# Attention and a gated feed-forward block on one core: an early dummy exponential and a new order table

## The chip, the cores and the metric

The kernel runs on one core of a Trainium2 chip. The metric is the device time of one execution in microseconds; the number compared is the median of several runs.

## What is computed

There are 4 batches of 12 heads; a sequence has 448 positions, a head 64 channels. Causal attention gives X (448 x 768 per batch), and X goes through a feed-forward block whose hidden values (1024) are gated by a convolution of three taps along the sequence. All in float32.

```python
scores = scale * np.matmul(q, k.transpose(0, 1, 3, 2))
scores = np.where(mask, -1000000000.0, scores)
attn = np.exp(scores - np.max(scores, axis=-1, keepdims=True))
attn = attn / (np.sum(attn, axis=-1, keepdims=True) + 1e-09)
out = np.matmul(attn, v)                      # 12 heads side by side are x
...
h = np.maximum(x @ w_in, 0.0)                 # 768 -> 1024
conv_out = sum over k of conv_w[k] * h shifted by k - 1 along the sequence
gate = 1.0 / (1.0 + np.exp(-conv_out))
return (h * gate @ w_out)                     # 1024 -> 768
```

## The kernel before

**Pairs of heads.** Work goes by pairs of heads, 24 of them, six to a batch, numbered from 0. A pair is five kinds of steps. TensorE makes transposed scores in blocks of 64 queries (`scores`, line 457) into four PSUM banks, as a whole or in two halves. VectorE adds the mask and takes the row minimum of the negated scores (`least`, line 492; in the trace a custom instruction and a read of its accumulator). ScalarE takes the exponential and the row sums (`expo`, line 498). TensorE transposes the probabilities (line 557) into the two banks of the ring `PT`, and ScalarE or VectorE copies them out (line 566). TensorE then multiplies with V (`times_v`, line 587). In the first batch the division by the row sums is applied to the product, by way of small matmuls that spread the reciprocals (line 603); in the others to the probabilities (line 529, "normalisation" below), after a sum (line 514) and a reciprocal (line 517). Two halves of the product are copied out and added (lines 646 and 650). From batch 1 on the product takes the two `PT` banks, so that the next transposes wait until both are copied out.

**Float32 at the speed of a rounded format.** Each operand of the feed-forward block is split into a rounded first part (lines 329, 330 and 333 for ScalarE, VectorE and POOL) and a second part, the rest (line 344, VectorE or POOL); a product is three matmuls of 448 columns, high by high, high by low, low by high. The weights come in 16 chunks each of W_in and W_out through three or more buffers, are scaled (line 369) and put together (line 372) before they are split.

**Feed-forward.** A first product (`ffn1`, line 903) sums nine matmuls of a kind over six pairs of X, then come relu, three taps, tanh and the gate (`activate`, lines 919 to 939). A second product (`ffn2`, line 961) is 24 matmuls to an output tile; ScalarE copies it out (line 972) and SyncE stores it. Batch 0 and 1 run beside the attention of the next batches: 144 first and 144 second matmuls for each, called "products" below. Batches 2 and 3 share the first half in `joint` (line 783), which uses seven instead of eight block products: it needs sums of weights and sums of X blocks (line 680) and adds results from PSUM (line 820). The 288 second products of both come last.

**What sets the order.** All steps are given to `Plan`, which writes the program: `run` goes through the steps that can be issued, estimates for each when it could start on each engine that may do it (`LAG`, `OWN`, `EXTRA` and a cost in ns per step; steps marked `port` take turns at a modelled port that VectorE and POOL share), and issues the one with the lowest rank. A rank is the start plus a lateness that the step was given, plus an entry of the table `OFFSET`, by kind and number of the step. `FROM` holds the time from which an engine counts as free. `PACE` gives for each pair of the last two batches how many products must have been issued before its scores and its product with V may be (through `progress`). The program has no scheduler at run time: each engine runs its list in order and waits on semaphores. `setup` (line 308) fills the mask, the identity and zeros; eight matmuls on zeros keep TensorE at work meanwhile.

Of the kernel before, what the change touches and what calls it, by code (L numbers as in the profile page):

```python
# [14 lines left out]
AF = mybir.ActivationFunctionType  # L15
# [8 lines left out]
class Plan:  # L24
# [8 lines left out]
    OWN = {"PE": 0, "DVE": 115, "ACT": 145, "POOL": 40, "SP": 0}  # L33
    EXTRA = {"PE": 100, "POOL": 42}
    WEIGHT = {"DVE": 1.15, "ACT": 1.0, "POOL": 0.5}
    FROM = {"PE": 3800.0, "SP": 500.0}
    ISSUE = {}
    OFFSET = {
        "PT": {11: -250, 12: -19050, 14: 100, 16: -50, 18: -19350, 19: -350, 20: -100, 21: -19500, 22: -200, 23: 100, 5: -100,
            9: -2750},  # L40
        "after": {5: 12750},
        "c12": {1: 4050},
        "c21": {3: 1550},
        "c22": {0: 100, 2: 18700},
        "chain": {140: 20000, 159: 7950, 189: 18150, 19: 850, 191: 3250, 206: 5600, 21: 600, 218: 5750, 236: 14150, 25: 650,
            34: 2050, 51: 1550, 57: 4850, 8: 1600, 96: 12050},
        "cw": {0: 350},
        "exp": {0: -100, 10: -9650, 14: 150, 16: -11250, 19: -400, 20: 1100, 4: -50, 5: -12250, 7: 50, 9: -100},
        "g": {(1, 0): -50, (1, 1): 100, (1, 2): -100, (1, 5): -250, (1, 6): -950, (1, 7): -250, (2, 1): 50, (2, 5): -50, (2,
            7): 50, (3, 0): 2050, (3, 4): 5550, (3, 5): 4450, (3, 7): 20000},  # L50
        "least": {0: -8300, 10: 1050, 13: 250, 14: 1400, 18: 500, 21: -1000, 22: -10850, 23: -450, 6: -500, 8: 400, 9: 100},
# [11 lines left out]
        "raw": {14: 1200, 16: 4150, 18: 3500, 19: 4500, 2: 3500, 23: 3600, 4: 450, 6: 1250, 8: 1000, 9: 5450},  # L63
        "rb": {5: 150},
        "s1": {1: 1100, 2: -14050},
        "s3": {0: -13750, 1: 1350, 2: 1100},
        "s4": {0: 100, 1: -250, 2: -100, 3: 9550},
        "scores": {10: 100, 13: -350, 22: 1950, 4: -10400, 9: 100},
        "sum": {(3, 0): -100},
        "t1": {0: 400, 1: 250, 2: -13650},  # L70
        "t1f": {1: 550, 2: -500},
        "t2": {1: -150, 2: 200},
        "t2f": {1: -1950},
        "t3f": {1: -4000},
        "t4": {0: -7800, 1: -19500, 2: -2250},
        "t4f": {1: -6350},
        "u2": {2: 1250},
        "vraw": {19: -3300, 2: -6400, 22: 1550, 3: 700, 4: 800, 5: 5200, 6: -11550, 9: -700},
# [4 lines left out]
    }  # L83
    SWITCH = {(0, 1): 90, (0, 2): 90, (3, 1): 90, (3, 2): 90, (1, 2): 95, (2, 1): 95, (1, 0): 200, (2, 0): 200, (1, 3): 100, (2, 3): 100, (0, 3): 20}

# [131 lines left out]
def attn_ffn_kernel(ctx: ExitStack, tc: tile.TileContext, qk, v, w_in, conv_w, w_out, out):  # L217
# [8 lines left out]
    nc = tc.nc  # L226
    P = 128
    B, NPAIR, _, _, S = qk.shape
# [40 lines left out]
    negm = many(2, [P, 8], F32, "negm")  # L269
    ssum = many(2, [P, 8], F32, "ssum")  # L270
# [38 lines left out]
    def setup():  # L309
        nc.gpsimd.memset(bank_zeros, 0.0)  # L310
        idle(bank[7], 8)
        nc.gpsimd.memset(mask, 0.0)
        for j in range(2):
            last = mask[64 * j : 64 * j + 64, S - 64 : S]
            nc.gpsimd.affine_select(
                out=last, in_=last, compare_op=ALU.is_ge, fill=-1.0e30,
                base=0, pattern=[[-1, 64]], channel_multiplier=1,
            )
        make_identity(nc, ident)
        for t in tops:  # L320
            nc.vector.memset(t, 0)
        for t in plan.rings["hr"]:
            nc.vector.memset(t[0][:, 0:1], 0.0)
            nc.vector.memset(t[0][:, S + 1 : S + 2], 0.0)
# [660 lines left out]
    LATE = 100  # L985
    SUM_LATE = 300
    PACED1 = False
    PACE = [-90 + 24 * i for i in range(2 * NPAIR + 1)]
    IN_AT = [(2, 3, 4, 4, 5)[i * 5 // NW] for i in range(NW)]
    OUT_AT = [i * NPAIR // NW for i in range(NW)]  # L990
    with tc.manual_schedule():
# [66 lines left out]
```

## Time and profile before

| what | value |
|---|---|
| median of 3 runs | 380.22 us (380.15 to 380.59) |
| the profiled execution | 381.26 us, of which 379.5 us are the span of the trace |
| mean granted TensorE clock | 0.998 of full speed |
| TensorE busy | 365.5 us, 96% of the span |
| VectorE, ScalarE, POOL busy | 279.3, 253.1, 158.2 us |
| DMA | 37.55 MB, 99 GB/s on the mean |

A share of busy time is an average over stages with different limits; which wait counts is read from the stage in which it stands. A wait is put down to the event that came last by the profile. In the rows L498 is line 498 of the kernel before; the kernel with the change has the same code four lines higher behind the setup (L494).

### The profile page before, as it was taken

How to read it: one execution, taken by the hardware profiler on the slowest of the kernel's cores; microseconds unless marked ns; L12 is line 12 of the kernel's file. 1: busy time of each engine (PE TensorE's matmuls, PEld its weight loads, DVE VectorE, ACT ScalarE, POOL GpSimd, SP SyncE). 2: the span in 40 equal slices, each digit the busy share in tenths (PEclk: the TensorE clock that was granted, in tenths of full speed). 3: DMA queues.
4: the chain of work that ended last, by engine and by line, in shares of the span. 5: the costliest groups of instructions: out<-in, count | busy, mean ns of one | idle time of the engine just before them, and what ended most of it. 6: DMA issues, size and time to landing. Idle time of an engine off the chain costs nothing.

```text
span 379.5 us, 8931 instructions
## 1 busy us (share of the span) xinstructions
PE 365.5 (96%) x3367; PEld 305.9 (81%) x3367; DVE 279.3 (74%) x762; ACT 253.1 (67%) x697; POOL 158.2 (42%) x187
## 2 busy tenths in 40 slices
PE   7999998999999999999999999899899899999996
PEld 3767766798898887888887888778699799999995
DVE  4788868878888767787968677769989898645500
ACT  2899898999871578978889988479544246434121
POOL 2257676545530042334247895841113902314600
PEclk9999999999999999999999999999999999999999
DMA  8997114342565252231204331310000000111021
GB/s 275 406 355 247 57 44 139 113 140 83 156 208 188 74 162 66 84 134 36 80 4 146 104 122 42 107 61 26 3 0 0 2 0 0 50 48 50 2 97 48
DMA packets 15163, 37.55 MB, mean 99 GB/s; under 512 B 1808, under 2 KB 4880, under 8 KB 15120
## 3 DMA queue, kind: packets, MB, share of 16 engines
q1 hardware_dynamic: 15120, 36.99, 28.8%
q8 instruction: 26, 0.43, 0.5%
q14 instruction: 17, 0.14, 0.1%
HBM read 31.47 MB, written 5.51 MB: 97 GB/s over the span
## 4 chain that ended last, share of the span: by engine, by line
PE 60%; DVE 14%; ACT 11%; issue 6%; POOL 5%; DMA 3%; POOLq 0%; ACTq 0%; DVEq 0%; SPq 0%
PE bank L961 23%; PE bank L903 9%; PE bank L557 7%; PE bank L587 7%; PE bank L457 7%; PE bank L783 6%; ACT p L498 4%; DMA wraw<-in_w_out_dram 3%; ACT parts L329 2%; DVE u L926 2%; DVE bank L492 2%; POOL wol L344 2%; DVE top L680 1%; POOL parts L344 1%; DVE parts L344 1%
## 5 line engine op out<-in xcount | busy, mean ns | idle before, releaser
L961 PE MATMUL bank<-parts,woh 128*128 128x448 f32 x384 | 112.7, 371 | 0.5 <-DVE woh L330 0.5
L498 ACT ACTIVATE p<-bank,negm 128x192 f32<-128x192 f32 (+6 forms) x168 | 78.9, 490 | 9.1 <-DVE negm L492 7.8
L961 PEld LDWEIGHTS bank<-parts,woh 128*128 128x128 f32 x384 | 71.0, 188 | 6.3 <-DVE woh L330 0.8
L492 DVE CUSTOM_DVE_ANT_0 bank<-bank,mask 128x384 f32<-128x384 f32 (+6 forms) x168 | 66.2, 452 | 7.5 <-PE bank L457 7.0
L961 PE MATMUL bank<-parts,wol 128*128 128x448 f32 x192 | 70.9, 369 | 0.0
L903 PE MATMUL bank<-parts,wih 128*128 128x448 f32 x192 | 58.4, 377 | 0.1
L557 PE MATMUL bank<-ident,p 128*128 128x128 f32 x336 | 51.0, 279 | 5.2 <-ACT p L498 1.9
L344 POOL TENSOR_TENSOR parts<-u,parts 128x448 fp32r<-128x448 f32 x37 | 43.8, 1188 | 19.9 <-ACT parts L329 17.8
L926 DVE SCALAR_TENSOR_TENSOR u<-hr,cw,u 128x448 f32<-128x448 f32 x64 | 45.8, 731 | 6.2 <-ACT u L939 5.3
L557 PEld LDWEIGHTS bank<-ident,p 128*128 128x128 f32 x336 | 38.3, 140 | 14.7 <-issue 3.3
L566 ACT COPY pt<-bank 128x512 f32<-128x512 f32 (+1 forms) x74 | 38.5, 541 | 14.8 <-PE bank L557 13.4
L457 PE MATMUL bank<-raw 64*64 64x128 f32 (+5 forms) x768 | 46.9, 362 | 0.6 <-DVE u L623 0.6
L333 POOL TENSOR_SCALAR parts<-u 128x448 fp32r<-128x448 f32 x21 | 12.9, 614 | 81.2 <-DVE u L932 45.1
L783 PE MATMUL bank<-parts,wih 128*128 128x448 f32 x150 | 42.9, 367 | 1.4 <-DVE hr L814 1.4
L587 PE MATMUL bank<-pt,vraw 64*64 64x64 f32 (+3 forms) x960 | 43.1, 317 | 0.0
L587 PEld LDWEIGHTS bank<-pt,vraw 64*64 64x64 f32 x960 | 31.0, 133 | 15.0 <-issue 8.2
L457 PEld LDWEIGHTS bank<-raw 64*64 64x64 f32 x768 | 30.2, 135 | 14.5 <-issue 7.2
L961 PEld LDWEIGHTS bank<-parts,wol 128*128 128x128 f32 x192 | 36.1, 188 | 3.2 <-DVE wol L344 0.5
L903 PEld LDWEIGHTS bank<-parts,wih 128*128 128x128 f32 x192 | 35.0, 188 | 3.0 <-DVE parts L344 0.3
L529 ACT ACTIVATE p<-p,rcp 128x256 f32<-128x256 f32 (+6 forms) x75 | 34.8, 514 | 3.7 <-DVE rcp L517 3.6
L498 ACT ACTIVATION_READ_ACCUMULATOR p<-bank,negm 128x1 f32 x168 | 36.9, 219 | 0.0
L903 PE MATMUL bank<-parts,wil 128*128 128x448 f32 x96 | 36.1, 376 | 0.0
(90 smaller groups left out, 549.5 us busy)
## 6 DMA issues: line engine op xcount, KB each, us to landing
raw<-in_qk_dram SPq DMA_DIRECT2D x24, 448.0 KB, 4.7
vraw<-in_v_dram SPq DMA_DIRECT2D x24, 320.0 KB, 3.0
wraw<-in_w_in_dram SPq DMA_DIRECT2D x16, 383.8 KB, 7.3
wraw<-in_w_out_dram SPq DMA_DIRECT2D x16, 383.8 KB, 3.5
out_dram<-u SPq DMA_DIRECT2D x24, 224.0 KB, 1.9
wraw<-in_conv_w_dram SPq DMA_DIRECT2D x1, 23.8 KB, 4.9
```

What stands on the lines that cost most here:

```text
L344: engine.tensor_tensor(out=out(), in0=src(), in1=f32(hi()), op=ALU.subtract)
L457: nc.tensor.matmul(at(s)[half(j ^ (k in SWAPPED)), to : to + k1 - k0], lhsT=t[:, 1, 64 * k : 64 * k + 64], rhs=t[:, 0, k0:k1], start=True, ...
L492: nc.vector.tensor_tensor_reduce(out=t, in0=t, in1=mask[:, S - 64 : S - 64 + n] if k == 2 else mask[:, S - n : S], scale=-0.125, scalar=3. ...
L498: nc.scalar.activation(at(t)[:, h : h + n], at(s)[:, o : o + n], AF.Exp, bias=negm[g % 2][:, c : c + 1], scale=-1.0, accum_out=ssum[g % 2] ...
L529: mul(t, t, rcp[g % 2][:, c : c + 1])
L557: nc.tensor.matmul(to, lhsT=p, rhs=ident, is_transpose=True)
L566: copy(at(part)[:, o : o + n], at(pt)[:, :n])
L587: nc.tensor.matmul(at((pv, r))[half(j), q0:q1], lhsT=at(vraw)[half(r), c if c < 3 else 3 + (c - 3) // 2, j], rhs=t[half(r), :, j], start=c ...
L783: nc.tensor.matmul(at(bank)[:, :S], lhsT=weights(w)[:, c], rhs=at(operands[c])[:, part], start=q == 0, stop=q == len(prods) - 1,)
L903: nc.tensor.matmul(at(ph)[:, :S], lhsT=block(w, NCC * f + cc), rhs=at(x)[:, part], start=q == 0, stop=q == len(prods) - 1)
L926: nc.vector.scalar_tensor_tensor(out=t, in0=src, scalar=w, in1=t, op0=ALU.mult, op1=ALU.add)
L961: nc.tensor.matmul(at(po)[:, :S], lhsT=block(w, NF * m + f), rhs=at(g)[:, part], start=q == 0, stop=q == len(prods) - 1)
```

## The change

Three things change. In `setup` VectorE sets the 8 columns of `negm[0]` to zero and ScalarE takes their exponential into `ssum[0]`, which later instructions overwrite. `PACE` starts 30 later and rises by 22 instead of 24 for each pair. The table `OFFSET` is another one throughout, and `FROM` lets the plan count ScalarE as free from 3500 ns on. Costs, lags and rules of the plan are the same.

```diff
-    FROM = {"PE": 3800.0, "SP": 500.0}
+    FROM = {"PE": 3800.0, "SP": 500.0, "ACT": 3500.0}
     ISSUE = {}
     OFFSET = {
-        "PT": {11: -250, 12: -19050, 14: 100, 16: -50, 18: -19350, 19: -350, 20: -100, 21: -19500, 22: -200, 23: 100, 5: -100,
-            9: -2750},
...
+        "PT": {10: -100, 11: 250, 14: -500, 15: -11650, 18: -11650, 19: 200, 20: -150, 21: -100, 6: -7550},
...
         make_identity(nc, ident)
+        nc.vector.memset(negm[0], 0.0)
+        nc.scalar.activation(ssum[0], negm[0], AF.Exp)
         for t in tops:
...
-    PACE = [-90 + 24 * i for i in range(2 * NPAIR + 1)]
+    PACE = [-60 + 22 * i for i in range(2 * NPAIR + 1)]
```

The order moves on every engine. Over the program VectorE's list is 23 instructions shorter, ScalarE's 11 and POOL's 14 longer; SyncE has the same number, TensorE's matmuls are the same in number and kind. Three places follow, in which p is a tile of probabilities, negm and ssum the row minima and sums, pt the copied transposes, parts the split X, wih and wil the two parts of W_in.

ScalarE, the first instructions of the program; before:

```order
L498 ACT_TABLE_LOAD
L498 ACTIVATE p_0_239,ssum_131<-bank_135,negm_129 128x448
L498 ACTIVATE p_0_238,ssum_131<-bank_136,negm_129 128x384
L498 ACTIVATE p_0_232,ssum_131<-bank_136,negm_129 128x128
L498 ACTIVATE p_0_236,ssum_131<-bank_137,negm_129 128x320
```

and with the change:

```order
L315 ACT_TABLE_LOAD
L315 ACTIVATE ssum_131<-negm_129 128x8
L494 ACTIVATE p_0_239,ssum_131<-bank_135,negm_129 128x448
L494 ACTIVATE p_0_238,ssum_131<-bank_136,negm_129 128x384
L494 ACTIVATE p_0_232,ssum_131<-bank_136,negm_129 128x128
L494 ACTIVATE p_0_236,ssum_131<-bank_137,negm_129 128x320
```

The one table load stands now ahead of the dummy exponential, and none is left in front of the first exponential of pair 0.

TensorE, behind the product of pair 5 with V; before, the first scores of pair 7, the first transposes of pair 6, the other scores of pair 7:

```order
L457 MATMUL bank_136<-raw 64x448 x2
L457 MATMUL bank_138<-raw 64x384 x2
L457 MATMUL bank_138<-raw 64x128 x2
L557 MATMUL bank_139<-ident,p_0_238 128x2x64
L557 MATMUL bank_139<-ident,p_0_239 128x128
L557 MATMUL bank_139<-ident,p_0_238 128x2x64
L557 MATMUL bank_139<-ident,p_0_239 128x128
L457 MATMUL bank_135<-raw 64x256 x2
L457 MATMUL bank_137<-raw 64x320 x2
L457 MATMUL bank_135<-raw 64x64
L457 MATMUL bank_135<-raw 64x128
```

and with the change, behind the second scores of pair 6:

```order
L899 MATMUL bank_141<-parts,wih_66 128x448 x2
L899 MATMUL bank_141<-parts,wil_82 128x448
L899 MATMUL bank_142<-parts,wih_68 128x448 x2
L899 MATMUL bank_142<-parts,wil_84 128x448
L453 MATMUL bank_137<-raw 64x448 x2
L453 MATMUL bank_138<-raw 64x384 x2
L453 MATMUL bank_138<-raw 64x128 x2
L899 MATMUL bank_142<-parts,wih_68 128x448 x2
L899 MATMUL bank_142<-parts,wil_84 128x448
L899 MATMUL bank_141<-parts,wih_66 128x448 x2
L453 MATMUL bank_136<-raw 64x256 x2
L453 MATMUL bank_135<-raw 64x320 x2
```

First feed-forward products stand now ahead of and between the scores of pair 7, and the transposes of pair 6 come after them.

ScalarE, from the end of the exponentials of pair 22 (tiles p_0) on; before:

```order
L498 ACTIVATE p_0_236,ssum_131<-bank_136,negm_129 128x64
L498 ACTIVATE p_0_239,ssum_131<-bank_138,negm_129 128x192
L529 ACTIVATE p_0_234<-p_0_234,rcp_133 128x256
L529 ACTIVATE p_0_239<-p_0_239,rcp_133 128x192
L972 ACTIVATE u_249<-bank_142 128x448
L646 COPY keep<-bank_139 128x448
L566 COPY pt<-bank_139 128x512
L566 COPY pt<-bank_140 128x512
```

and with the change:

```order
L494 ACTIVATE p_0_236,ssum_131<-bank_135,negm_129 128x64
L494 ACTIVATE p_0_239,ssum_131<-bank_136,negm_129 128x192
L525 ACTIVATE p_1_237<-p_1_237,rcp_134 128x320
L525 ACTIVATE p_1_235<-p_1_235,rcp_134 128x256
L525 ACTIVATE p_1_237<-p_1_237,rcp_134 128x64
L525 ACTIVATE p_0_236<-p_0_236,rcp_133 128x320
L525 ACTIVATE p_0_234<-p_0_234,rcp_133 128x256
L525 ACTIVATE p_0_236<-p_0_236,rcp_133 128x64
L525 ACTIVATE p_0_239<-p_0_239,rcp_133 128x192
L562 COPY pt<-bank_140 128x512
L562 COPY pt<-bank_139 128x512
```

The copy of pair 20's product (keep) is no longer in ScalarE's list there; VectorE makes it, right behind a reciprocal of pair 22. ScalarE has three normalisations of pair 21 (p_1) there.

## Rows read from the trace of the kernel before

**Rows 1.** The page's first part: busy us (share), instructions of each engine.
```profile
PE 365.5 (96%) x3367; PEld 305.9 (81%) x3367; DVE 279.3 (74%) x762; ACT 253.1 (67%) x697; POOL 158.2 (42%) x187
```

**Rows 2.** Busy time by stretch: stretch, length, busy us (instructions) of each engine.
```profile
10.00:62.00 52.00, 49.55 (x757) 36.71 (x758) 42.54 (x147) 45.98 (x147) 29.97 (x39) 1.00 0.62 222
62.00:120.00 58.00, 58.00 (x462) 50.06 (x461) 48.02 (x120) 46.97 (x128) 25.95 (x28) 1.00 0.45 139
120.00:245.00 125.00, 124.18 (x1343) 102.54 (x1342) 95.11 (x315) 97.50 (x295) 59.73 (x72) 1.00 0.28 91
245.00:296.00 51.00, 46.88 (x361) 39.32 (x360) 44.89 (x90) 33.27 (x77) 15.16 (x16) 1.00 0.05 17
```

**Rows 3.** The chain that ended last: start us, us, what.
```profile
317.57 58.39 PE bank L961 x288
```

**Rows 4.** Timeline, 5 to 12 us: start, us, engine, line, operation [idle before].
```profile
7.32 1.28 ACT L498 ACT_TABLE_LOAD   x1 [7.32 <-DVE negm L492]
...
8.62 0.63 ACT L498 ACTIVATE p<-bank,negm 128x448 f32<-128x448 f32 x1
...
10.05 0.63 PE L557 MATMUL bank<-ident,p 128*128 128x128 f32 x4 [1.88 <-ACT p L498]
```

**Rows 5.** Timeline of TensorE, 50 to 66 us.
```profile
54.64 1.76 PE L587 MATMUL bank<-pt,vraw 64*64 64x384 f32 x40
...
58.87 1.03 PE L457 MATMUL bank<-raw 64*64 64x256 f32 x20 [0.56 <-DVE u L623]
60.30 1.13 PE L557 MATMUL bank<-ident,p 128*128 128x128 f32 x8 [0.40 <-ACT p L529]
```

**Rows 6.** Timeline, 244 to 248 us, VectorE, ScalarE and TensorE.
```profile
244.69 0.18 DVE L517 RECIPROCAL rcp<-rcp 128x4 f32<-128x4 f32 x1
...
246.15 0.52 ACT L646 COPY keep<-bank 128x448 f32<-128x448 f32 x1
...
246.73 1.25 PE L557 MATMUL bank<-ident,p 128*128 128x128 f32 x8 [1.35 <-ACT keep L646]
```

**Rows 7.** Waits of TensorE: who for whom, us, times, longest.
```profile
PE bank L783 <- DVE hr L814: 1.4, 1, 1.4
...
PE bank L783 <- DVE keep L820: 1.2, 1, 1.2
```

**Rows 8.** Groups of ScalarE by shape: count, busy us, mean ns, idle before.
```profile
L566 ACT COPY pt<-bank 128x512 f32<-128x512 f32 x57 | 32.6, 589 | 13.6 <-PE bank L557 12.4 <-DVE negm L492 0.8
...
L369 ACT ACTIVATE top<-wraw 128x384 f16<-128x384 bf16 x23 | 14.9, 654 | 8.4 <-DMA wraw<-in_w_out_dram 8.4
...
L566 ACT COPY pt<-bank 128x256 f32<-128x256 f32 x17 | 6.4, 379 | 1.2 <-PE bank L557 1.0
...
L329 ACT CAST wih<-wraw 128x384 fp32r<-128x384 f32 x7 | 3.8, 559 | 0.0
...
L646 ACT COPY u<-bank 128x448 f32<-128x448 f32 x6 | 3.2, 527 | 1.5 <-PE bank L587 0.9 <-POOL wol L344 0.7
```

**Rows 9.** Groups of VectorE by shape.
```profile
L924 DVE TENSOR_SCALAR u<-hr,cw 128x448 f32<-128x448 f32 x15 | 8.3, 552 | 11.5 <-ACT hr L919 8.7 <-DMA out_dram<-u 1.7 <-POOL parts L344 0.9
...
L344 DVE TENSOR_TENSOR parts<-u,parts 128x448 fp32r<-128x448 f32 x7 | 4.8, 691 | 1.4 <-ACT parts L329 1.3
L529 DVE TENSOR_SCALAR p<-p,rcp 128x320 f32<-128x320 f32 x9 | 4.5, 495 | 0.3
L680 DVE TENSOR_TENSOR top<-top,wil 128x384 f32<-128x384 f32 x6 | 4.1, 686 | 0.0
...
L344 DVE TENSOR_TENSOR parts<-keep,parts 128x448 fp32r<-128x448 f32 x3 | 3.5, 1179 | 0.2
...
L566 DVE COPY pt<-bank 128x256 f32<-128x256 f32 x7 | 2.9, 417 | 1.7 <-PE bank L557 1.1 <-ACT p L498 0.6
...
L330 DVE CAST wih<-u 128x384 fp32r<-128x384 f32 x2 | 0.7, 360 | 0.1
...
L804 DVE COPY keep<-bank 128x448 f32<-128x448 f32 x1 | 0.6, 611 | 0.0
```

More of the change, by code (lines that the diff above doesn't have):

```diff
@@ L35 @@
     WEIGHT = {"DVE": 1.15, "ACT": 1.0, "POOL": 0.5}
-    FROM = {"PE": 3800.0, "SP": 500.0}
+    FROM = {"PE": 3800.0, "SP": 500.0, "ACT": 3500.0}
     ISSUE = {}
     OFFSET = {
-        "PT": {11: -250, 12: -19050, 14: 100, 16: -50, 18: -19350, 19: -350, 20: -100, 21: -19500, 22: -200, 23: 100, 5: -100,
-            9: -2750},
[L41 to L46, printed above, removed]
-        "cw": {0: 350},
[L48 to L51, printed above, removed]
[11 rows of a table removed]
[L63 to L78, printed above, removed]
[4 rows of a table removed]
@@ new lines @@
+        "PT": {10: -100, 11: 250, 14: -500, 15: -11650, 18: -11650, 19: 200, 20: -150, 21: -100, 6: -7550},
+        "after": {5: 9100},
+        "c12": {0: 1950},
+        "c22": {1: 550, 2: 6050, 3: 19800},
+        "chain": {114: 6500, 142: 9650, 187: 20000, 197: 1800, 206: 7100, 215: 9600, 231: 7300, 29: 3150, 61: 7000},
+        "cw": {0: 350},
+        "exp": {0: -400, 1: 100, 11: 300, 12: 2650, 14: -100, 16: -6850, 17: -2150, 18: -18750, 20: -3000, 21: -8700, 22: -50,
+            23: 450, 4: -9450, 5: 600},
@@ new lines @@
+        "g": {(0, 1): -250, (1, 1): 150, (1, 2): 300, (1, 5): -50, (1, 7): -50, (2, 1): -150, (2, 2): 200, (2, 3): 150, (3,
+            1): -200, (3, 4): 9800, (3, 5): 16500},
+        "least": {10: -450, 15: -2000, 16: -6900, 17: -500, 21: 450, 4: 150, 5: 150, 9: -250},
[11 rows of a table added]
+        "raw": {3: -12900, 4: 250, 5: 3750, 8: 550, 9: -1150},
+        "rb": {1: -4300, 3: -15800},
+        "s2": {1: 150, 2: -300, 3: -100},
+        "s3": {0: -16000, 3: 100},
+        "s4": {0: 150, 1: 100, 3: 14550},
+        "scores": {16: -20000, 18: -14750, 4: 100, 5: 100, 6: -4750},
@@ L83 @@
+        "sum": {(1, 0): 950, (1, 1): -500, (1, 3): 150, (2, 2): -6650, (2, 3): -100, (3, 1): 1450, (3, 3): -6050},
+        "t1": {2: -450},
+        "t3": {0: -10350, 1: 150},
+        "t4f": {0: 2700, 1: 450},
+        "u2": {0: 700},
+        "vraw": {1: 650, 2: 150, 22: 5000, 3: -850, 4: 3800, 5: 650, 7: 250},
[4 rows of a table added]
     }
```

30 rows, old and new, of the table OFFSET are left out of this document.

## The prediction

> **What bounds the kernel now.** I read the engines' shares first. TensorE is busy for 365.5 of 379.5 us, 96% [rows 1]; nothing else is near that. Its work is the same before and after: equal counts of scores, transposes, products with V and feed-forward products. So a new order can only change the time in which TensorE stands still. The second view, busy time by stretch, tells where that is [rows 2]: 2.45 us in 10 to 62 us, none in 62 to 120, 0.82 in 120 to 245, and 4.12 in 245 to 296. The first 10 us hold a start-up wait, shown below; and the last part, the second feed-forward halves of the last two batches, is 288 products in 58.39 us, one behind the other [rows 3]. That is 0.203 us each, which I take for a product below.
>
> What kind of waits these are is in TensorE's list of waits and in the timelines. In the start, ScalarE gets the first row minima, then spends 1.28 us on its table, and only then begins the first exponential at 8.62; TensorE has waited 1.88 us when the first transposes start at 10.05 [rows 4]. In the first batch TensorE has little beside attention, since a feed-forward unit needs X of all six pairs; ScalarE (45.98 of 52 us) and VectorE (42.54) set the pace [rows 2]. At 58.87 and 60.30 TensorE stops for 0.56 and 0.40 us [rows 5]. Around 246 us the transposes of pair 21 wait 1.35 us for a PSUM bank that ScalarE copies out late [rows 6]. In the joint part TensorE waits twice for VectorE, 1.4 and 1.2 us [rows 7], while VectorE works 44.89 of 51 us [rows 2].
>
> **The change part by part.** The sum is made against the profiled execution: 379.5 us of span and 1.76 around it make 381.26; the median of the runs shown is 380.22, so I take a difference from the one and subtract it from the other.
>
> *Dummy exponential.* It adds an 8-column memset on VectorE and an 8-column exponential on ScalarE, both while these wait for the first scores; cover is ScalarE's 7.3 idle us ahead of the load. The load moves with it (the order has one load in each kernel). The load began when VectorE's first minima came, at 7.32 [rows 4]; without it the first exponential can start there, 1.28 us earlier, and the transposes behind it as well: their wait of 1.88 has room for all of that. I take 1.28. Bounds: 1.28, and 0 if something else of the first pairs ends last behind it.
> That is by the row: the exponential starts 0.02 us after the load's end. The Trainium skill, "ScalarE: Activation LUTs", section "What ACT_TABLE_LOAD costs", counts a drain of about 1.38 us beside the 1.283 us load for each switch of table; by it, as an estimate, the move would save 2.66 us. The trace has the load's 1.28 and shows no such drain, so the sum keeps 1.28.
>
> *First batch (pairs 0 to 5).* Ahead of the last exponential of pair 5, ScalarE now has one rounding of a weight less (0.559), one scaling of a raw weight less (0.654), two copies of transposes less (0.589 and 0.379), but two copies of a product more (2 x 0.527) [rows 8]: 2.18 - 1.05 = 1.13 us less. VectorE's list ahead of it shrinks more. With the 1.28 the product of pair 5 could stand 2.4 us before its 54.64 [rows 5]. But TensorE also has less to run until then: 21 first feed-forward products instead of 30 (9 x 0.203 = 1.83), and the second half of pair 6's scores comes behind the product (1.03 by the same twenty matmuls in [rows 5], about 0.96 as start to next start). 2.8 less work, 2.4 less time: idle up to pair 5's product **+0.4 us**. This is the term I know least. If only the 1.28 of the table is passed on, it is 2.8 - 1.3 = +1.5; if VectorE's shorter list counts, -1.0.
>
> *Pairs 6 and 7.* The two waits above came when the transposes of pair 6 followed at once on pair 7's first scores. Now 6 and 5 feed-forward products (11 x 0.203 = 2.2 us) stand between the scores there, ahead of the transposes. 0.96 us of idle can be covered: **-1.0**. Bounds -1.0 and 0 (the wait only moves, for instance to the 50 products' start).
>
> *62 to 245 us.* TensorE is nearly full and stays so [rows 2]; feed-forward products and attention are only dealt out differently, and the new pace holds pair 12's scores until 85 output products of the first batch have run. POOL takes 4 more second parts of W_out and 4 more of its roundings. What hides that is that these products now come later against attention: 85 of the 144 stand ahead of pair 12's scores, 143 before. **0**; if that cover is gone, a chunk of W_out comes later by what POOL is slower.
>
> *Around 246 us.* Pair 20's product was copied out by ScalarE at 246.15, behind pair 22's exponentials, two normalisations and an output copy, and the transposes followed at 246.73, though VectorE's reciprocals were through at 244.87 [rows 6]. Now VectorE makes the copy right behind that reciprocal, and the addition after it: at about 0.6 each, as the copy of the same size in [rows 9], they end at 246.1, and the transposes can follow 0.6 to 0.7 us earlier; and 32 instead of 30 products stand in front (0.4). ScalarE has three normalisations of pair 21 instead, no longer than that. Wait 1.35 - 1.1: **-1.1**. Bounds -1.35 and 0.
>
> *Joint part.* Ahead of pair 23's scores TensorE has run 277 instead of 273 of the second batch's output products, so 4 x 0.203 = 0.8 us less is left to cover what comes behind. VectorE's list from the last row minimum to its first bank addition (line 820) loses two splits (2 x 0.691), a copy of transposes (0.417), a copy of a first half (0.611), a tap (0.552) and a rounding (0.360), and gains four normalisations (about 4 x 0.495) and a sum of weights (0.686) [rows 9]: 3.3 - 2.7 = 0.65. These means hold waits, as the spread of one kind shows (the two rows of splits); two of the normalisations are also of smaller sizes. I take 1.0. +0.8 - 1.0 = **-0.2**. Bounds: +0.8, and -2.6 if both waits go.
>
> Sum: +0.4 - 1.0 - 1.1 - 0.2 = -1.9 us; 381.26 becomes 379.4 and the median 380.22 becomes **378.3 us**.
>
> **The rivals.** *Slower: the first batch's pace stays.* The mechanism is the first term: if ScalarE, VectorE and POOL need as long for pairs 1 to 5 as before, TensorE with 2.8 us less work just waits; +1.5 there. Idle grows from the point where pair 5's product starts later than 51.8 us (54.64 - 2.8), and with the forecast's other terms (-2.3) the kernel is slower from 54.1 on. If softmax is so late, pair 6's waits come back behind the new products as well (0 instead of -1.0), a late pair 20 leaves -0.3 of the 1.1, and the joint part wins only 0.65 against its 0.8: +1.5 - 0.3 + 0.1 = +1.3, 381.5. For it: ScalarE is not the only pace setter there. Against it: it is the busiest, and its list is shorter.
> *No difference.* The gain of the start is eaten in the first batch (+0.4 to +1.0), and one of the later waits stays: about -0.3, 379.9. For it speaks that TensorE's idle moved between stages comes back as idle elsewhere.
> *More gain.* In the joint part VectorE's two-input instructions are stretched by POOL: an addition into parts takes 1.179 us on the mean where another of the same size takes 0.691 [rows 9]. A table whose order keeps POOL and VectorE apart there removes both waits: -2.6 instead of -0.2, -4.3 in all, 375.9. Against it: POOL has as many instructions there as before.
> *The load has a hidden price.* If moving the load takes away as much again as the load itself (1.28) in waiting that the rows give to others in the first pairs, the sum is -3.2: 377.0. The 0.02 us in the row speak against it. That is about what the Trainium skill's page on ScalarE, named above, would make of it with its drain.
>
> **How the numbers follow.** The forecast (-0.9 to -3.0) has 0.45, more gain 0.15, no difference 0.20, slower 0.17, the hidden price 0.03. The predicted time is the likeliest case's. About 0.2% (0.76 us) is what a measurement of this kernel can tell. Faster by more than that: 0.44 of the forecast's 0.45, and 0.18 of two rivals, less a little for bounds, 0.61. Slower by more: 0.17. Within: 0.22. The range takes in the nearer half of the bigger gain and of the slower case, and leaves out some 0.08 on either side: 376.2 to 381.2; the likeliest case alone has 377.2 to 379.3.
>
> **What would show it.** Right: a table load that ends before 3 us, the first exponential near 7.3 and the first transposes near 8.8; pair 5's product by about 52 to 53 us with no wait over 0.4 us in the next 8 us; transposes of pair 21 with a wait under 0.4 us; the 1.4 and 1.2 us waits of the joint part together within 0.5 us of before; TensorE's busy time unchanged within 1 us. Wrong: an idle of TensorE in 10 to 62 us that is larger than 2.45 by over 1 us; a new wait over 1 us between 62 and 245 (W_out's parts on POOL would be the first to look at); or a joint part in which TensorE waits longer for VectorE.

## The result and the profile after

The kernel after takes 374.67 us (median of 4 runs, 374.62 to 376.02) beside 380.32 of the kernel before: a ratio of 0.9859 (95% interval 0.9837 to 0.9882), that is 5.4 us less (4.5 to 6.2). It is faster, as forecast, but by nearly three times the forecast 1.9 us, and below the range. The two profiled executions, which the following compares, are 381.26 and 374.62 us; they lie 6.6 us apart, 1.2 more than the runs, so the stretches below add up to more than the gain. In what follows a gain in us is a ratio times the time of before beside it.

The page's first part, kernel after (busy us, share, instructions of each engine; before: [rows 1]):

```profile
PE 364.5 (98%) x3367; PEld 305.5 (82%) x3367; DVE 265.0 (71%) x739; ACT 258.9 (69%) x708; POOL 164.4 (44%) x201
```

TensorE's work is what it was. VectorE is busy for 14.3 us less. Its shorter list is the smaller part of that: by an estimate from the traces (below), 11.1 us of it are time in which its instructions were held by POOL.

Busy time by stretch, kernel after (as [rows 2]):

```profile
10.00:62.00 52.00, 50.78 (x742) 37.07 (x742) 43.70 (x151) 48.41 (x150) 30.37 (x37) 1.00 0.65 232
62.00:120.00 58.00, 58.00 (x562) 48.73 (x561) 43.79 (x123) 55.09 (x154) 32.34 (x38) 1.00 0.45 137
120.00:245.00 125.00, 123.71 (x1256) 104.05 (x1255) 89.65 (x286) 91.09 (x273) 62.77 (x80) 1.00 0.28 89
245.00:296.00 51.00, 50.42 (x374) 43.72 (x373) 45.94 (x97) 32.07 (x71) 17.38 (x16) 1.00 0.05 17
```

In the last row TensorE stands still for 0.58 us instead of 4.12. Timeline of the start, kernel after (as [rows 4]):

```profile
0.72 1.28 ACT L315 ACT_TABLE_LOAD   x1 [0.72 <-PEq L1038]
2.01 0.21 ACT L315 ACTIVATE ssum<-negm 128x8 f32<-128x8 f32 x1
7.02 0.63 ACT L494 ACTIVATE p<-bank,negm 128x448 f32<-128x448 f32 x1 [4.80 <-DVE negm L488]
...
8.45 0.63 PE L553 MATMUL bank<-ident,p 128*128 128x128 f32 x4 [0.55 <-ACT p L494]
```

The load is over at 2.00; the first transposes come 1.60 us earlier, 1.28 of it the table, the rest because the first scores, begun at 4.6 us in both, were through 0.26 us sooner in this execution. TensorE, 49 to 77 us, kernel after (as [rows 5]; the two products are those of pairs 5 and 6):

```profile
49.05 1.79 PE L583 MATMUL bank<-pt,vraw 64*64 64x384 f32 x40
...
58.97 0.69 PE L899 MATMUL bank<-parts,wih 128*128 128x448 f32 x2 [0.48 <-ACT hr L915]
...
60.24 0.66 PE L553 MATMUL bank<-ident,p 128*128 128x128 f32 x4 [0.39 <-ACT p L525]
...
76.54 1.76 PE L583 MATMUL bank<-pt,vraw 64*64 64x384 f32 x40
```

Pair 5's product stands 5.6 us earlier, and behind it new waits take the place of those of [rows 5]. TensorE's waits, kernel after (as [rows 7]):

```profile
PE bank L553 <- DVE u L646: 1.3, 1, 1.3
...
PE bank L899 <- ACT hr L915: 0.5, 1, 0.5
...
PE bank L779 <- DVE hr L810: 0.3, 1, 0.3
```

The 1.2 us of the joint part and the 1.35 us at 246 us are gone, of the 1.4 us 0.3 are left; a new one of 1.3 us has come, at 123.4 us. The chain that ended last, kernel after (as [rows 3]): TensorE alone from 268.73 to 369.3, first products of the joint part, then the same 288 as before.

```profile
268.73 42.22 PE bank L779 x207
310.94 58.38 PE bank L957 x288
```

So that no shift of work between stretches deceives, I take TensorE's **lost time**: the moment at which a piece of work ends, less the plain time of all that TensorE has done until then (0.202 us a wide product, 1.51 the 32 score matmuls, 1.69 the 40 with V, 0.109 a transpose, and so on, from runs of each without a gap). The differences between two kernels hardly depend on these values; the levels do.

| lost until the end of | before | after | difference |
|---|---|---|---|
| pair 0's product | 5.5 | 3.9 | -1.6 |
| pair 5's product | 10.0 | 7.2 | -2.8 |
| what precedes batch 0's first output product | 13.1 | 11.3 | -1.8 |
| pair 22's scores | 19.1 | 16.1 | -3.0 |
| pair 21's transposes | 21.3 | 16.3 | -5.0 |
| the joint part | 25.7 | 19.05 | -6.6 |

The gain is made in three places: the start, 62 to 237 us a little, and from 237 us on the most.

### The profile page after: what moved, and what is told of

Same layout as the page of the kernel before. It is cut to its first block, busy times and chain, and to the rows that moved or that the text cites. A ratio compares the mean times of both kernels' runs of the same rounds, so it can differ in the third digit from the quotient of the medians.

```text
span 372.8 us, 8941 instructions
## 1 busy us (share of the span) xinstructions
PE 364.5 (98%) x3367; PEld 305.5 (82%) x3367; DVE 265.0 (71%) x739; ACT 258.9 (69%) x708; POOL 164.4 (44%) x201
## 4 chain that ended last, share of the span: by engine, by line
PE 86%; ACT 5%; DVE 4%; issue 2%; DMA 1%; POOL 1%; SPq 0%; ACTq 0%; DVEq 0%; POOLq 0%
PE bank L957 30%; PE bank L899 14%; PE bank L779 11%; PE bank L553 10%; PE bank L583 10%; PE bank L453 9%; ACT p L494 2%; DMA wraw<-in_w_out_dram 1%; PE bank L599 1%; PE bank L301 1%; ACT p L525 1%; DVE u L676 1%; DVE top L676 1%; DVE keep L676 0%; ACT u L968 0%
## 5 line engine op out<-in xcount | busy, mean ns | idle before, releaser
L957 PE MATMUL bank<-parts,woh 128*128 128x448 f32 x384 | 113.9, 371 | 0.0
L494 ACT ACTIVATE p<-bank,negm 128x320 f32<-128x320 f32 (+6 forms) x168 | 78.1, 483 | 17.2 <-DVE negm L488 16.1
L488 DVE CUSTOM_DVE_ANT_0 bank<-bank,mask 128x384 f32<-128x384 f32 (+6 forms) x168 | 66.2, 454 | 11.4 <-PE bank L453 11.3
L340 POOL TENSOR_TENSOR parts<-u,parts 128x448 fp32r<-128x448 f32 x38 | 45.9, 1212 | 39.5 <-ACT parts L325 38.0
L899 PE MATMUL bank<-parts,wih 128*128 128x448 f32 x192 | 57.2, 376 | 0.5 <-ACT hr L915 0.5
L922 DVE SCALAR_TENSOR_TENSOR u<-hr,cw,u 128x448 f32<-128x448 f32 x64 | 46.8, 739 | 9.6 <-ACT u L935 8.9
L453 PE MATMUL bank<-raw 64*64 64x128 f32 (+5 forms) x768 | 46.0, 359 | 0.0
L779 PE MATMUL bank<-parts,wih 128*128 128x448 f32 x150 | 42.9, 367 | 0.3 <-DVE hr L810 0.3
L525 ACT ACTIVATE p<-p,rcp 128x448 f32<-128x448 f32 (+6 forms) x90 | 40.8, 511 | 1.6 <-DVE rcp L513 1.5
L562 ACT COPY pt<-bank 128x512 f32<-128x512 f32 (+1 forms) x61 | 32.5, 550 | 12.7 <-PE bank L553 11.9
L329 POOL TENSOR_SCALAR parts<-u 128x448 fp32r<-128x448 f32 x20 | 11.9, 597 | 66.2 <-DVE u L928 50.4
L494 ACT ACTIVATION_READ_ACCUMULATOR p<-bank,negm 128x1 f32 x168 | 35.8, 213 | 0.0
```

The costliest lines, as they stand in the source:

```text
L340: engine.tensor_tensor(out=out(), in0=src(), in1=f32(hi()), op=ALU.subtract)
L453: nc.tensor.matmul(at(s)[half(j ^ (k in SWAPPED)), to : to + k1 - k0], lhsT=t[:, 1, 64 * k : 64 * k + 64], rhs=t[:, 0, k0:k1], start=True, ...
L488: nc.vector.tensor_tensor_reduce(out=t, in0=t, in1=mask[:, S - 64 : S - 64 + n] if k == 2 else mask[:, S - n : S], scale=-0.125, scalar=3. ...
L494: nc.scalar.activation(at(t)[:, h : h + n], at(s)[:, o : o + n], AF.Exp, bias=negm[g % 2][:, c : c + 1], scale=-1.0, accum_out=ssum[g % 2] ...
L525: mul(t, t, rcp[g % 2][:, c : c + 1])
L562: copy(at(part)[:, o : o + n], at(pt)[:, :n])
```

## The experiments

### The dummy exponential alone

```diff
 (kernel before)
         make_identity(nc, ident)
+        nc.vector.memset(negm[0], 0.0)
+        nc.scalar.activation(ssum[0], negm[0], AF.Exp)
```

> The kernel before with the two lines of the dummy exponential and nothing else. Carried through (prediction's first term alone): the first exponential begins near 7.3 us and the 1.28 us of the table come off the whole time, 380.3 - 1.3 = 379.0 us. Eaten in the first batch (its pace is set by ScalarE and VectorE from other reasons, or a later wait takes it): 380.3 to 380.0. A hidden price of the load: 377.7.

Measured: 0.9974 (0.9959 to 0.9989), -1.0 us. The counterpart takes the two lines out of the kernel after:

> The kernel after without the dummy exponential, its order kept. Carried through: 374.7 + 1.3 to 1.6 (the exponential began 1.60 us earlier in the profiled run) = 376.0 to 376.3 us. If the gain of the first 62 us comes from the order alone and the table's load was hidden or absorbed: 374.7 to 375.0. If the order was fitted to the early table and breaks without it: above 376.8.

Measured: 0.9892 (0.987 to 0.9913), -4.1 us against before, where after has -5.4: the dummy is worth 1.25 us there (0.1 to 2.4, by the two intervals). Both agree with the 1.28 of the load: it is carried through from the first pair to the end, in either order.

### Parts of the new order in the old one

For these the program is planned twice without issuing anything, once by the table and pace of before and once by the new ones; then it is issued in the one recorded order up to the step that makes a key, and in the other from there. In the traces VectorE, ScalarE and POOL run the list of the version named first up to the cut. In the names N is the new order and O the old, for the stretch up to batch 0's first output product, the one up to the first joint product, and the rest.

```diff
+    SEGMENTS = (("new", (("po", 0, 0), 1)), ("old", None))      # splice_NOO
+    SEGMENTS = (("old", ("chain", 1)), ("new", None))           # splice_OON
+    SEGMENTS = (("new", ("chain", 1)), ("old", None))           # splice_NNO
```

> New order (with the dummy) up to the first output product of batch 0, from there the order of before (a step that the order of before has earlier is issued at once at the cut). Theory A, every stretch gives what TensorE's own waits say: -1.8 us, 378.5. Theory B, the early gain is only a shift of feed-forward work and is given back at the cut: 380.0 to 380.8. Theory C, the prediction's terms for this stretch (+0.4 - 1.0): -0.6, 379.7.

Measured: 0.9975 (0.9961 to 0.9988), -1.0 us, the same as the dummy alone. The lost time before the first output product is 11.88 us here and 11.86 in the kernel before with the dummy. So the new order of the first 93 us gives nothing of its own that these runs could tell from noise (some 0.5 us): what it wins up to pair 5's product it gives back up to there. Theory C gave the time by luck, with two terms that were both wrong.

> Order of before (no dummy) up to the first product of the joint feed-forward part, from there the new order. Theory A, the stretches add up: the two waits of 1.4 and 1.2 us go and other small ones come, -1.7 us, 378.6. Theory B, the joint part of the new order only fits to what its own earlier part leaves behind (pair 23's scores 4 us earlier): VectorE's list is as late as before, waits of 1 to 2.6 us stay, 380.0 to 381. Theory C, the prediction's term: -0.2, 380.1.

Measured: 1.0081 (1.0052 to 1.011), **+3.1 us**. A case that no theory had: the new joint part behind the old past is worse than the old one. TensorE's list of waits in splice_OON:

```profile
PE bank L846 <- DVE keep L883: 3.0, 1, 3.0
```

and VectorE's timeline ahead of it, where it waits for ScalarE between the steps of one feed-forward unit, one unit behind the other (that this makes the addition late is read from the rows; no run tried it):

```profile
278.21 0.63 DVE L995 SCALAR_TENSOR_TENSOR u<-u,hr 128x448 f32<-128x448 f32 x1 [0.65 <-ACT u L992]
279.47 0.62 DVE L408 TENSOR_TENSOR parts<-u,parts 128x448 fp32r<-128x448 f32 x1 [0.63 <-ACT parts L393]
280.83 1.41 DVE L989 SCALAR_TENSOR_TENSOR u<-hr,cw,u 128x448 f32<-128x448 f32 x2 [0.74 <-ACT u L1002]
```

> New order with the dummy up to the first product of the joint part, from there the order of before. Stretches add up: the joint part costs its old 1.7 us more than in the new order, 374.7 + 1.7 = 376.4 us. If the joint part's gain is only what the earlier stretches leave behind: 374.7 to 375.2. If the old joint part does not fit what it finds (as the new one did not fit the old state, +3 us): 377.5 or more.

Measured: 0.9932 (0.9907 to 0.9957), -2.6 us: the last answer. At the first joint product splice_NNO is 5.3 us of lost time ahead of before; it loses 1.8 of that again by the end of its old joint part. The stretches don't add up; a list is fitted to what the list before it leaves.

### What holds VectorE: gates for POOL

The reading behind these runs. Groups of VectorE by shape in the kernel before, 235 to 240 us, just ahead of the wait of [rows 6]:

```profile
L529 DVE TENSOR_SCALAR p<-p,rcp 128x384 f32<-128x384 f32 x1 | 1.2, 1159 | 0.0
L529 DVE TENSOR_SCALAR p<-p,rcp 128x192 f32<-128x192 f32 x1 | 1.1, 1126 | 0.0
L529 DVE TENSOR_SCALAR p<-p,rcp 128x256 f32<-128x256 f32 x1 | 1.1, 1087 | 0.0
L529 DVE TENSOR_SCALAR p<-p,rcp 128x128 f32<-128x128 f32 x1 | 1.0, 1044 | 0.0
...
L529 DVE TENSOR_SCALAR p<-p,rcp 128x320 f32<-128x320 f32 x1 | 0.4, 373 | 0.0
```

The same groups from 150 to 190 us:

```profile
L529 DVE TENSOR_SCALAR p<-p,rcp 128x384 f32<-128x384 f32 x2 | 0.8, 422 | 0.0
L529 DVE TENSOR_SCALAR p<-p,rcp 128x128 f32<-128x128 f32 x3 | 0.8, 280 | 0.0
...
L529 DVE TENSOR_SCALAR p<-p,rcp 128x256 f32<-128x256 f32 x1 | 0.3, 348 | 0.0
```

One kind of instruction, 280 or 1044 ns for the same 128 columns. Timeline of POOL in the kernel before, same place:

```profile
235.44 1.00 POOL L344 TENSOR_TENSOR s<-u,s 128x384 fp32r<-128x384 f32 x1
236.41 1.14 POOL L680 TENSOR_TENSOR top<-wih,wih 128x384 f32<-128x384 f32 x1
237.63 2.23 POOL L680 TENSOR_TENSOR top<-top,wil 128x384 f32<-128x384 f32 x2
```

Of the four long ones three begin within an instruction of POOL, the fourth 0.01 us before one; all end 0.1 to 0.2 us after it: the 1044 ns run from 236.59 to 237.63, POOL's sum ended at 237.55. The short one, 128 x 320, begins at 237.56, between two instructions of POOL. In the joint part, VectorE and POOL in the kernel before (two lists of one timeline):

```profile
290.38 0.56 DVE L680 TENSOR_TENSOR top<-top,wil 128x384 f32<-128x384 f32 x1
290.86 1.39 DVE L344 TENSOR_TENSOR wil<-u,wih 128x384 fp32r<-128x384 f32 x1
292.17 1.37 DVE L680 TENSOR_TENSOR top<-top,wil 128x384 f32<-128x384 f32 x1
293.46 1.36 DVE L344 TENSOR_TENSOR wil<-top,wih 128x384 fp32r<-128x384 f32 x1
294.75 1.67 DVE L820 TENSOR_TENSOR keep<-bank,keep 128x448 f32<-128x448 f32 x3
...
290.50 1.33 POOL L680 TENSOR_TENSOR u<-wih,wih 128x384 f32<-128x384 f32 x1 [8.37 <-ACT wih L329]
291.91 2.50 POOL L680 TENSOR_TENSOR u<-u,wil 128x384 f32<-128x384 f32 x2
```

Three instructions of 0.55 us take 1.36 to 1.39 under POOL's sums, 2.5 us more in all, right ahead of the bank addition of line 820 that TensorE awaits for 1.2 us [rows 7]. The additions that read a bank (1.67 us for three, under POOL's next instructions) are not held: three take 1.68 us in g2_joint below. This is what the Trainium skill, "SBUF — State Buffer", section "Who interferes with whom", says: VectorE shares one pair of ports with GpSimd (POOL); a VectorE instruction in a two-port mode, or with two SBUF inputs while GpSimd reads SBUF, contends for it, and of whichever comes second it says that it "fully blocks". The trace agrees, with the numbers above. Summed over all VectorE instructions, the time beyond the lower quartile of the same kind and size (where over 0.12 us) is 24.1 us in the kernel before and 13.0 in the kernel after; 10.9 and 3.5 of it lie in 120 to 245 us, 4.3 and 1.8 in 245 to 296. Of the 42 instructions so counted before, 40 begin within an instruction of POOL and two at most 0.04 us ahead of one; of the 27 after, all begin within one.

That shows holds, not what they cost: most may lie where nothing waits for VectorE. So the next runs keep the order of before on every engine and add to POOL up to four one-column reads, which make a POOL instruction wait until VectorE's instruction is done:

```diff
 (kernel before)
+    look = lambda src: nc.gpsimd.tensor_scalar_add(gate_out, src()[:, :1], 1.0e-9)
+    plan.gates = {      # POOL's step: what it reads first
+        (("sum", (1, 2)), 1): lambda: look(lambda: at(("tile", 21, HOME[2][0]))[:, HOME[2][1] :]),       # gates_246
+        (("t3", 1), 1): lambda: look(lambda: f32(at(("t2", 1))[:, 1])),              # gates_joint
+        (("t2", 2), 1): lambda: look(lambda: f32(at(("t3", 2))[:, 1])),              # gates_joint
+        (("sum", (3, 3)), 1): lambda: look(lambda: f32(wi_lo[5][:, 0])),             # gates_joint
+    }
```

> The order of before, all of it; one thing is added: POOL reads one column of the last tile that VectorE normalises for pair 21 before it starts a weight sum, so that the sum (1.14 us from 236.41 in the trace of before, two more behind it) can't lie under VectorE's normalisations from 235.51 to 239.99. Port theory: these normalisations take 0.25 to 0.45 us each instead of 1.04 to 1.16, pair 22's minima start near 238.3 instead of 239.91, the copy of pair 20's product and the transposes of pair 21 come 1.3 to 1.6 us earlier, TensorE's wait of 1.35 us before them goes: 380.5 - 1.4 = 379.1 us. Order theory (the copy is late because of its place in ScalarE's list, not because of held normalisations): the wait stays above 1 us, 380.2 to 380.8.

> The order of before; three gates in the joint part: a split of POOL may start only when VectorE's split that began 0.5 us later in the trace is done (261.66 and 271.89 us), and POOL's last weight sums only when VectorE's three operations from 290.86 to 294.8 are done. Port theory: VectorE gets back up to 0.6 + 0.8 + 2.5 us, TensorE's waits of 1.42 us (at 273.9) and 1.21 us (at 295.4) go, 380.5 - 2.6 = 377.9 us, or 378.5 if the delayed sums of POOL cost a new wait. Order theory (VectorE's list is as long as before and its place decides): both waits stay, 380.2 to 381.5.

> The order of before with the four gates and the dummy exponential, nothing of the new table and pace. Port theory: 1.0 of the table + 1.4 + 2.6 = -5.0 us, 375.5, nearly the kernel after. Order theory: only the dummy's, 379.5.

Measured: 1.0008 (0.9995 to 1.0021), 0.9985 (0.9968 to 1.0001) and 0.9899 (0.9871 to 0.9926): +0.3, -0.6 (both within noise) and -3.8 us. By the totals the port theory had lost two of three. The chains said otherwise: in gates_246 pair 21's transposes came with 1.4 us less lost, as expected, yet the 288 last products took 59.53 us instead of 58.39. The tile that the gate writes had been put ahead of the tiles of the rings and had moved them all by 32 bytes. The same three with that tile behind all others:

```diff
-    gate_out = sb.tile([P, 1], F32, name="gate_out")            # ahead of the rings
+    gate_out = ctx.enter_context(tc.tile_pool(name="gate", bufs=1)).tile([P, 1], F32, name="gate_out")   # behind them
```

> The gate of gates_246 again, with its one-column result tile put behind all other tiles, so that no other tile moves by 32 bytes. In gates_246 TensorE's feed-forward products took 206 to 207 ns instead of 203 in the whole run. If the displacement caused that: 203 ns here, and the 1.37 us that the gate won by the joint part come through to the end: 380.5 - 1.3 = 379.2 us. If the gate itself slows the products, or the joint part eats the gain (its first wait stays 1.4 us): 380.2 to 381.

> The three gates of the joint part with the tile behind all others. Port theory: products at 203 ns, the wait at 295.4 gone, of the one at 273.9 some 0.7 us left (as in gates_joint): 380.5 - 1.9 to 2.6 = 377.9 to 378.6 us. If the holds at the port only hide other lateness: 380 or more.

> Order of before, four gates with the tile behind all others, and the dummy. Additive: 1.0 to 1.3 + 1.3 + 2.2 = -4.6, 375.9 us; with less product time than gates_all_dummy by about 1000 x 3.5 ns where TensorE is full, 374.0 to 375. If it lands at the 376.7 of gates_all_dummy, the displacement meant nothing.

Measured: g2_246 0.9962 (0.9949 to 0.9976), **-1.4 us**; g2_joint 0.9959 (0.9946 to 0.9971), **-1.6**; g2_all_dummy 0.9891 (0.9875 to 0.9906), **-4.2**. The parts add up (1.4 + 1.6 + 1.0 = 4.0). The third missed its own expectation: 376.61 us is 0.1 less than gates_all_dummy, not 0.8 to 2.7, so this pair alone would not show that the displacement costs anything; the rows of the last products and the runs with an unused tile (below) do. The sum of held time is no measure of the gain either: in g2_all_dummy it is still 21.3 us, 2.8 less than before, while the gates gain 3 us. Timeline of VectorE in g2_246; in the kernel before the same five normalisations took 4.48 us, and the first minimum of pair 22 began at 239.91:

```profile
235.06 2.14 DVE L613 TENSOR_SCALAR p<-p,rcp 128x384 f32<-128x384 f32 x5
237.87 0.63 DVE L576 CUSTOM_DVE_ANT_0 bank<-bank,mask 128x448 f32<-128x448 f32 x1 [0.67 <-PE bank L541]
```

of TensorE, whose transposes of pair 21 now follow on the products without a wait:

```profile
244.93 2.25 PE L641 MATMUL bank<-ident,p 128*128 128x128 f32 x13
```

and of POOL, which waits 1.29 us and makes no engine later by it:

```profile
237.29 0.22 POOL L371 TENSOR_SCALAR gate_out<-p 128x1 f32<-128x1 f32 x1 [1.29 <-DVE p L613]
237.58 1.02 POOL L763 TENSOR_TENSOR top<-wih,wih 128x384 f32<-128x384 f32 x1
```

So the wait at 246 us began here: held normalisations, pair 22's minima 2 us later (1.6 of it counted from the start of the normalisations), its exponentials later, behind them on ScalarE the copy of pair 20's product, behind that the transposes. VectorE in g2_joint, the three instructions from above:

```profile
289.94 0.55 DVE L430 TENSOR_TENSOR wil<-u,wih 128x384 fp32r<-128x384 f32 x1
290.41 0.55 DVE L765 TENSOR_TENSOR top<-top,wil 128x384 f32<-128x384 f32 x1
290.88 0.55 DVE L430 TENSOR_TENSOR wil<-top,wih 128x384 fp32r<-128x384 f32 x1
291.35 1.68 DVE L905 TENSOR_TENSOR keep<-bank,keep 128x448 f32<-128x448 f32 x3
```

TensorE's wait for the bank addition is gone, the other one is 0.8 us. Lost time at the end of the joint part is 3.3 us less than in the kernel before. Of that, 2.1 us arise within the joint part; the other 1.2 stand ahead of the gates, most of them in 93 to 237 us, where traces of one order differ by as much. 0.8 is given back at the first output products behind the joint part, which wait for the last unit's parts.

### The pace

With the table of before, the new pace gives the order of before unchanged, on every engine; it never decides there. Nor does the new entry of `FROM`: without it the kernel after has the same lists. The other way round:

```diff
 (kernel after)
-    PACE = [-60 + 22 * i for i in range(2 * NPAIR + 1)]
+    PACE = [-90 + 24 * i for i in range(2 * NPAIR + 1)]
```

> The kernel after with the pace of before (the other way round there is nothing to run: with the table of before, the new pace gives the order of before unchanged). If the pace is a part of the gain by itself: 376 to 378 us. If only the table counts: 374.3 to 375.2. If table and pace are fitted to each other, as the joint part was to its past: 378 us or more, with new waits of TensorE in the joint part.

Measured: 1.0772 (1.0729 to 1.0815), **+29 us**, with waits of TensorE for parts and splits in all of the last two batches, the longest 3.2 us. Not all of it is waiting: TensorE is busy for 380.2 us instead of 364.5, and its granted clock, 1.00 in the kernel after, is 0.97 on the mean in 120 to 245 us and 0.89 in 296 to 350. So the third answer: a table and its pace are one thing, and no share of the gain belongs to either.

### A better place for three steps

In the kernel after, VectorE stands behind a transfer while TensorE waits for an addition that could be made. Timeline, VectorE and TensorE, kernel after:

```profile
120.78 0.39 DVE L365 TENSOR_SCALAR top<-wraw 128x384 f16<-128x384 bf16 x1 [1.37 <-DMA wraw<-in_w_out_dram]
...
122.74 0.55 DVE L646 TENSOR_TENSOR u<-bank,u 128x384 f32<-128x384 f32 x1
...
123.44 0.63 PE L553 MATMUL bank<-ident,p 128*128 128x128 f32 x4 [1.29 <-DVE u L646]
```

```diff
 (order of after, three steps put ahead of the narrowing of W_out's part 9)
+    AHEAD_OF = [((("xs", 10), 1), (("w", 1, 9, 0), 0)), (("p", 11, 0), (("w", 1, 9, 0), 0)), (("p", 11, 2), (("w", 1, 9, 0), 0))]
```

> The kernel after, with three of VectorE's steps (the addition of pair 10's product and two small normalisations of pair 11) put ahead of the narrowing of a W_out part, for whose DMA VectorE waits 1.37 us at 119.4 to 120.8 in the trace of after. If that place in the list causes TensorE's 1.29 us wait at 123.4: 374.7 - 1.2 = 373.5 us. If the next wait takes it (W_out's part, the transposes' copies on ScalarE): 374.4 to 375.

Measured: 373.27 us, 0.9813 (0.9792 to 0.9833) against before, where after has 0.9859. The transposes now begin at 121.99 without a wait. Timeline of VectorE in after_moved, the addition ahead of the narrowing:

```profile
119.33 0.55 DVE L722 TENSOR_TENSOR u<-bank,u 128x384 f32<-128x384 f32 x1
...
120.63 0.40 DVE L442 TENSOR_SCALAR top<-wraw 128x384 f16<-128x384 bf16 x1 [0.36 <-DMA wraw<-in_w_out_dram]
```

### The place of the tiles

```diff
 (before_pad32; 16 columns for 64 bytes, 24 for 96, 32 for 128)
+    pad = sb.tile([P, 8], F32, name="pad")
     plan = Plan()
```

> The kernel before, with an unused tile of 32 bytes ahead of the tiles of the rings: nothing else. If the place of the tiles alone made the products slow in gates_246, gates_joint and gates_all_dummy: 206 to 207 ns each here as well, and the time up by 0.2 us (the last 288 products alone give 1.1 us, the rest where TensorE is full) to 3 us. If the gates themselves did it: 203 ns and 380.5 us.

> As before_pad32 with 64 bytes. If what counts is the place within 64 bytes: 203 ns, 380.5 us. If any displacement against the weights slows the products: 206 ns or more. A faster product (under 203 ns) would show that the place in before was not the best.

Measured: 1.0039 (1.0024 to 1.0054), +1.5 us, and 0.9967 (0.9953 to 0.9981), -1.3 us, for tiles that nobody touches. The chain's last row, before_pad32:

```profile
317.07 59.53 PE bank L962 x288
```

before_pad64:

```profile
317.36 57.62 PE bank L962 x288
```

The displaced tiles, not the gates, slowed the products of the first three gate runs. On the fastest order:

> after_moved with an unused tile of 64 bytes ahead of the rings. The products took 200 to 201 ns instead of 203 in before_pad64; if that holds here, where TensorE is nearly always full: 288 last products give 0.6 us, all 1044 up to 2.5: 373.3 - 0.6 to 2.5 = 370.8 to 372.7 us. If the gain was the other order's: 373.3.

> The same with 96 bytes. If the product's time has a period of 64 bytes: like 32 bytes, 206 to 207 ns, 374.5 to 376. If it falls and rises over 128 bytes: between 200.5 and 203 ns or lower, 371 to 373.3 us.

> The same with 128 bytes. If the period is 128 bytes: 203 ns and 373.3 us, as without a pad. If not, another value, which the last 288 products show.

Measured: **370.81 us** with 64 bytes, 0.9726 (0.9708 to 0.9744), the fastest of all; 375.78 with 96 and 374.57 with 128 bytes. The 288 products take 57.62, 59.15 and 58.76 us there, 58.38 without a pad. No simple period: 128 bytes are not the same as none.

## Why the prediction was wrong in size, step by step

- **Dummy, -1.28: right.** -1.0 and -1.25 in the two runs. The load ended at 2.00 us; the first exponential began at 7.02. No hidden price: neither run allows a gain of 2.6 us.
- **First batch, +0.4, and pairs 6 and 7, -1.0: both wrong, nearly cancelling.** Up to pair 5's product TensorE lost 2.8 us less (predicted: 0.4 more, bounds +1.5 and -1.0), because pair 5's product came at 49.05, not at 52 to 53. I had counted what leaves ScalarE's list and called VectorE's list a bound only; which of the two brought the product forward no run shows. Behind it the waits did not go but came anew (0.48 and 0.39, and smaller ones). Up to batch 0's first output product the sum is -1.8 in the trace against -0.6 predicted, and splice_NOO shows what lies beneath: -1.0 as the dummy alone, nothing by the order.
- **62 to 245 us, 0: about 1 us short, cause open.** The trace gives -1.2 up to pair 22's scores, in spite of a new wait of 1.3 us (one of the prediction's own signs of being wrong). Traces of one order differ here: the order of before lost 1.0 us less in this stretch in g2_joint than in the kernel before, whose wait of 0.5 us for a part of W_out was absent there. But over seven traces with the order of before in this stretch (products not displaced) the loss from batch 0's first output product to pair 22's scores is 5.0 to 6.6 us, and over three with the new one 4.7 to 4.8; the means are 1.0 apart. VectorE's held time fell by 7.4 us in 120 to 245, but no run isolates that.
- **Around 246 us, -1.1: right in sign and place, half the size, and a nearer cause was missed.** Measured -2.0 in lost time. I explained the wait by the copy's place in ScalarE's list. g2_246 leaves that place alone, frees five normalisations at 235 to 240 us, and gains 1.4 us. The chain began where I had not looked. In the kernel after the copy is VectorE's, as forecast, and ends at 242.42, just ahead of the transposes; what that gives by itself no run isolates:

```profile
241.80 0.62 DVE L642 COPY keep<-bank 128x448 f32<-128x448 f32 x1 [0.83 <-PE bank L957]
...
242.62 1.17 PE L553 MATMUL bank<-ident,p 128*128 128x128 f32 x8
```

- **Joint part, -0.2: the step that failed.** Measured -1.6. I priced VectorE's list by mean durations of kinds, saw that "these means hold waits", and took 1.0. The means were of two populations, 0.55 and 1.37 us, and which one an instruction belongs to is set by what POOL does at that moment. An order can change that without removing any instruction; counting the list cannot see it. g2_joint: order unchanged, POOL's starts moved, -1.6 us.
- **Together.** By stretch the measured terms are -1.0 (start, by splice_NOO), -1.0, -2.0 and -1.6, in all -5.6 beside the 5.4 of the runs and the 1.9 of the forecast. The joint part is the largest single share of the shortfall, not the whole of it.
- **The rivals.** "More gain" named this mechanism, in the joint part and with a price of -2.4 beside the forecast; it got 0.15, and its time, 375.9, was the nearest of all. That is in part luck, since it took both waits of the joint part to go (-2.6) and nothing more at 246 us or before. The argument against it, that POOL has as many instructions there as before, was wrong: the number is not the point, the overlap is. Its mechanism, extended to 246 us, is worth 3.0 us on the kernel before (g2_246 and g2_joint); with the dummy that makes 4.2 of the 5.4 us. The trace of the kernel after shows the same at both places. Around 246 us VectorE has one normalisation left behind pair 22's minima, of 0.32 us, and ScalarE makes the other seven; one of 1.07 us ahead of the minima costs nothing, since these wait 1.12 us for their scores behind it. Ahead of the first bank addition of line 816 (820 before) VectorE makes the weight sums that were POOL's, while POOL stands idle for 8.45 us, and in that time its instructions with two SBUF inputs take 0.55 to 0.68 us:

```profile
286.93 0.55 DVE L340 TENSOR_TENSOR wil<-u,wih 128x384 fp32r<-128x384 f32 x1
...
287.22 1.27 POOL L340 TENSOR_TENSOR parts<-u,parts 128x448 fp32r<-128x448 f32 x1 [8.45 <-ACT parts L325]
```

  So the new table wins there by the same mechanism as far as its trace tells; no run puts the holds back into the kernel after, so the share of each us stays open.
- The slower rival had its condition (pair 5's product later than 51.8 us) clearly unmet.

## What to carry to other kernels

Where one kind of instruction on VectorE shows two durations, lay POOL's timeline beside it before taking a mean: the gap is a wait that an order, or a one-column read that gates POOL, can remove. It pays only where another engine waits for that instruction; the sum of such gaps does not tell. When such an experiment adds a tile, put it where no other tile moves, and look at a row that should not change (here 288 products without a gap) before believing a total. And a table of order is fitted as a whole: half of a better one can be worse than the old one.

## What the runs showed of the hardware

- In the rows above, VectorE's normalisations (SBUF to SBUF) and its instructions with two SBUF inputs took 1.04 to 1.39 us instead of 0.28 to 0.55 when they began within an instruction of POOL (one of them 0.01 us ahead); additions with one input from a bank took 1.67 us for three beside 1.68.
- TensorE's products of 128 x 448 took 200.1, 202.7, 204.0, 205.4 or 206.7 ns each (57.62 to 59.53 us for 288) with tiles displaced by 64, 0, 128, 96 or 32 bytes, at a granted clock of 1.00, the level of 2.4 GHz, from 315 to 365 us in all of them. By the order of allocation in the kernel, what moved were the tiles behind the pad, the rings with the moving operands among them, not the weights, which come ahead of it. What about the place matters was not found; between best and worst it is 3% of a product, on a kernel that TensorE fills to 98%.
